# The mean of a SoLU layer taken from the activations on GpSimd instead of from the weights, with the transposes and loads around it moved

## The chip, the cores and the metric

One core of a Trainium2 chip. The metric is the device time of one execution in microseconds (us), lower is better. A time is the median of its runs, with the lowest and the highest behind it.

## The reference

All inputs have 8 batches, 8 heads, 576 rows, 64 columns per head; `w_in` is 512 x 1024, `w_out` 1024 x 512.

```python
scores = scale * q @ k.T                       # per batch and head, 576 x 576
thresh = max(scores) - tau                     # scores below it are dropped
attn   = softmax of what is left
x      = attn @ v                              # 4608 tokens x 512
h      = x @ w_in
u      = h * softmax(h)                        # "solu" in the original
mu, var = mean(u), mean((u - mu) ** 2)         # per token, over 1024
out    = ((u - mu) / sqrt(var + 1e-6) * g_ln) @ w_out
```

The point is `mu`. It can be taken from `u` (once per tile of 128 tokens), or from the weights: if each column of `g_ln * w_out` has its own mean taken off, a constant in `u` adds nothing to the product, and `mu` need not be subtracted at all.

## The kernel before

The kernel runs 144 **rounds**. Each does the scores of one block of 128 rows for two heads, and beside them one step of the rest. In the steady state four rounds make a cycle; I call them a, b, c and d:

- a: scores, x times `w_in` (first half), weights times v
- b: scores, x times `w_in` (second half), weights times v
- c and d: scores, u times `w_out` (two halves), transposes of the next batch's q and k

One cycle is one tile of 128 tokens, and there are 36. The last of them run after the last scores: the tail. These are the parts that the change touches (cuts marked by `...`):

```python
    def add_up(c): ...        # VectorE: total of w_out's chunks
    def mean(): ...           # TensorE: ones/1024 times total
    def center():
        for c in range(NC):
            nc.vector.tensor_tensor(out=w2[:, c], in0=w2[:, c], in1=totals[0], op=ALU.subtract)
    ...
    def scores(s, items):
        ps = [ps_mm.tile([P, 1024], F32, tag=f"s{h}", name="s_ps") for h in range(2)]
        ...
        for n, make, keep in items:     # transposes of q, k or u into the tiles' spare columns
            make(spare, x)
        for ks in (slice(SM, S), slice(0, SM)):
            ...                         # the scores themselves
    ...
    def ff_stats(t):
        ...
        for f in range(2):
            nc.vector.bn_stats(out=bs[:, f], in_=u[:, 512 * f : 512 * f + 512])
        nc.vector.bn_aggr(out=mv, in_=bs)
        # then six small GpSimd operations that make the row scale rs
    ...
    LAG_PV = 3      # weights times v is due three rounds after the scores
    ...
        # one round: scores(+transposes), maxes, ramp, exps | normalise, ff_stats |
        #            step with w_in or w_out | weights times v | block transposes to wT
```

`wT` holds the transposed softmax weights. VectorE turns 32 x 32 blocks, and eight DMA transfers put the blocks in place, so weights times v depends on a transfer. PSUM is full: two tiles for scores (their last 448 columns take transposes), and two tiles, here called the pair, for everything else.

Of the kernel before, what the change touches and what calls it, by code (L numbers as in the profile page):

```python
# [16 lines left out]
P = 128  # L17
# [3 lines left out]
def kernel(  # L21
# [225 lines left out]

    totals = []

    def add_up(c):  # L250
        if c == 1:
            totals.append(work.tile([P, DM], F32, tag="ob", name="total"))
        if c:
            total = totals[0]
            nc.vector.tensor_tensor(
                out=total, in0=total if c > 1 else w2[:, 0], in1=w2[:, c], op=ALU.add
            )

    def mean():
        total = totals[0]  # L260
        ones = work.tile([P, P], F32, tag="ob", name="ones")
        nc.gpsimd.memset(ones, 1.0 / DFF)
        tag, m = take("mean")
        nc.tensor.matmul(out=m[:, 0:DM], lhsT=ones, rhs=total, start=True, stop=True)
        nc.scalar.copy(out=total, in_=m[:, 0:DM])
        pairs_free.append(tag)

    def center():
        for c in range(NC):
            nc.vector.tensor_tensor(out=w2[:, c], in0=w2[:, c], in1=totals[0], op=ALU.subtract)  # L270



# [115 lines left out]
    def scores(s, items):  # L389
        b, kind, hp, r = slots[s]  # L390
        ps = [ps_mm.tile([P, 1024], F32, tag=f"s{h}", name="s_ps") for h in range(2)]

        spare = dict(enumerate(ps), base=S, eased=s <= NW)
        x = 0
        kept = []
        for n, make, keep in items:
            make(spare, x)
            kept.append((keep, x))
            x += n
        for ks in (slice(SM, S), slice(0, SM)):  # L400
            for h in range(2):
                for y in range(2):
                    if kind < 2:
                        d = pairs[b * NP + hp]
                        t = P * (2 * kind + r) + 64 * y
                        lhsT = d["qT"][ROWS[h], t : t + 64]
                    else:
                        d = pairs[b * NP + r + 2 * y]
                        lhsT = d["qe"][ROWS[h]]
                    nc.tensor.matmul(  # L410
                        out=ps[h][ROWS[y], ks], lhsT=lhsT, rhs=d["kT"][ROWS[h], ks],
                        start=True, stop=True,
                    )
        live[s] = dict(ps=ps, kept=kept, spare=spare)

# [73 lines left out]
    def attend(key):  # L489
# [3 lines left out]
        unit["y"] = take("pv")  # L493
        _, y = unit["y"]
        y = y.rearrange("p (u n) -> p u n", u=2)

        for e in range(2) if kind == 2 else [None]:
            for m in range(NK):
                for u in range(2):
                    d, h0 = source(b * NP + (hp if e is None else e + 2 * u))  # L500
                    for h in range(2):
                        if e is None:
                            to = y[ROWS[h], u, 0:P].rearrange("p (r g x) -> p g r x", r=2, g=2)
                            rhs = wT[ROWS[u], :, m, :, h]
                        else:
                            to = y[ROWS[h], u, 64 * e : 64 * e + 64].rearrange(
                                "p (g x) -> p g x", g=2
                            )
                            rhs = wT[ROWS[u], :, m, e, h]
                        nc.tensor.matmul(  # L510
                            out=to, lhsT=d["v"][ROWS[u], h0 + h, m], rhs=rhs,
                            start=m == 0, stop=m == NK - 1,
                        )

    def attended(key):
# [73 lines left out]

    def ff_stats(t):  # L590
        d = ffn[t]
# [4 lines left out]
        for f in range(2):  # L596
            nc.vector.bn_stats(out=bs[:, f], in_=u[:, 512 * f : 512 * f + 512])  # L597
        nc.vector.bn_aggr(out=mv, in_=bs)  # L598


# [11 lines left out]
    def u_item(t, f):  # L612
# [14 lines left out]

        return 4, make, keep


# [74 lines left out]
    for s, (b, kind, hp, r) in enumerate(slots):  # L705
        if r == 1:
            pv_due.append((s + LAG_PV, (b, kind, hp)))

# [5 lines left out]
    for i in range(NP, NPAIR):  # L714
        b, hp = divmod(i, NP)
        at = 8 + 2 * hp if i < 2 * NP - 1 else PER * (b - 1) + (6 + 3 * hp if hp < 3 else PER - 1)
        preps += [
# [7 lines left out]
    for b in range(1, B):  # L725
        r = PER * (b - 1)
        load_at.setdefault(r + 2, []).append(lambda b=b: load_qk(b, 0))
        load_at.setdefault(r + 8, []).append(lambda b=b: load_qk(b, 1))
        load_at.setdefault(r + 9, []).append(lambda b=b: load_v(b, 0))
        load_at.setdefault(r + PER + 6, []).append(lambda b=b: load_v(b, 1))  # L730

    with tc.manual_schedule():
# [6 lines left out]
        load_v(0, 0)  # L739
        load_v(0, 1)  # L740
        nc.sync.dma_start(out=g_rows, in_=g_ln.rearrange("(c p) -> c p", p=P))
# [4 lines left out]
        pieces = {r: x for x, r in enumerate(range(16))}  # L746
        whole = {0: 1, 1: 2, 3: 3}

# [8 lines left out]
        while True:  # L757
# [14 lines left out]
            busy = cur is not None or prev is not None  # L772
            items = []
            if more:
                room = SPARE
                if u_due and u_due[0][0] <= rnd:
                    _, t, f = u_due.pop(0)
                    items.append(u_item(t, f))
                    room -= 4
# [13 lines left out]
            elif u_due and u_due[0][0] <= rnd:  # L793
                for _, t, f in u_due:
                    ff_t(t, f)
                u_due = []
            if rnd in whole:
# [3 lines left out]
            if rnd - 1 in pieces:  # L801
                weight_c(pieces[rnd - 1])
            if pieces.get(rnd - 3) == 2 * NP + NC - 1:
                mean()
            for job in middle.pop(rnd, []):
# [12 lines left out]
            if due and (step is None or step[0] == "h") and len(pairs_free) > (step == ("h", 0)):  # L818
                attending = pv_due.pop(0)[1]
            if step == ("h", 0):  # L820
                ff_h(cur, 0, rnd + 1 < NS)
                quarter = 1
            elif step == ("h", 1):
# [3 lines left out]
                late.setdefault(rnd + 1, []).append(lambda t=cur: ff_mul(t))  # L827
                middle.setdefault(rnd + 3, []).append(lambda t=cur: ff_stats(t))
            elif step == ("o", 0):
# [3 lines left out]
            elif step == ("o", 1):  # L833
# [3 lines left out]
                if cur is not None:  # L837
                    u_due += [(rnd + 1, cur, 0), (rnd + 2, cur, 1)]
                prev, cur = cur, None
                quarter = 0  # L840
            if attending is not None:
                attend(attending)
                begin.setdefault(rnd + 1, []).append(lambda key=attending: attended(key))
                b, kind, hp = attending
# [10 lines left out]
            if rnd in pieces:  # L855
# [4 lines left out]
                if x + 1 < len(pieces):  # L860
                    weight_a(x + 1)
            x = pieces.get(rnd - 2, -1) - 2 * NP
            if x > 0:
                add_up(x)
            if pieces.get(rnd - 3) == 2 * NP + NC - 1:
                center()
                w2_done = True
            rnd += 1
# [33 lines left out]
```

## Time and profile before

| | before |
|---|---|
| time in the first measurement, us | 963.13 (962.52 to 965.56) |
| TensorE busy | 892.6 us, 93% of the span |
| VectorE, ScalarE, GpSimd busy | 72%, 61%, 49% |
| start of round 46 / rounds 46 to 142 / rest, us | 306.2 / 569.8 / 84.2 |
| mean length of a, b, c, d between rounds 46 and 141, us | 6.87, 6.88, 5.02, 4.98: cycle 23.75 |

The granted clock is the share of its full clock that TensorE's throttle let through. The waits of TensorE from 200 to 940 us complete what the prediction shows of the first 200. Columns: who waits (engine, tile, line), for whom, then us in total, number, longest; "issue" means that the profile names nobody. Tiles: `s_ps` holds scores, `h_ps` x times `w_in`, `pv` weights times v, `o_ps` u times `w_out`, `tp` and `tp_u` transposes, `uT` the turned u.

```profile
PE tp_u L638 <- ACT uT L641: 2.6, 3, 0.9
PE pv L510 <- issue: 1.5, 1, 1.5
PE s_ps L283 <- ACT w L439: 1.3, 2, 0.7
PE s_ps L410 <- issue: 0.5, 1, 0.5
PE s_ps L283 <- ACT uT L624: 0.3, 2, 0.2
```

### The profile page before, as it was taken

The numbers are of one execution on the slowest core, as the hardware profiler recorded it, in microseconds if no ns is written. First come the engines' busy times: TensorE is split into PE (matmuls) and PEld (weight loads), VectorE is DVE, ScalarE is ACT, GpSimd is POOL, SyncE is SP. The second block draws the span as 40 slices with busy tenths as digits, with TensorE's granted clock in tenths as the row PEclk, the third lists the DMA queues.
The fourth block names the chain that finished last, engine by engine and source line by source line (L and its number), as shares of the span: only waits on it lengthen the run. The fifth ranks groups of instructions, "written<-read, shape, count | busy, mean of one in ns | idle before, by whom it ended". The sixth has DMA issues, their size and how long they took to land. (4 is left out here: it accounts for less than half of the span.)

```text
span 964.4 us, 42893 instructions
## 1 busy us (share of the span) xinstructions
PE 892.6 (93%) x18583; PEld 647.8 (67%) x18583; DVE 692.1 (72%) x1298; ACT 593.0 (61%) x1291; POOL 473.2 (49%) x899
## 2 busy tenths in 40 slices
PE   4467678999999999999999999999999999999997
PEld 2334445678768777787777886778867887655543
DVE  4797976777767777777777777777777777777221
ACT  5676754677666666666666666666666666665111
POOL 2867665445544555445544454445544555554111
PEclk9587689999999999999999999999999999999999
DMA  9969625774678447874678546874668445744200
GB/s 238 255 192 196 159 68 150 172 190 116 150 176 201 115 114 175 202 165 117 160 176 191 121 119 164 202 163 115 170 154 206 110 118 131 163 112 111 61 22 22
DMA packets 87037, 143.31 MB, mean 149 GB/s; under 512 B 28985, under 2 KB 61761, under 8 KB 86849
## 3 DMA queue, kind: packets, MB, share of 16 engines
q1 hardware_dynamic: 85616, 138.60, 60.1%
q8 instruction: 147, 2.41, 1.1%
q10 hardware_dynamic: 1232, 1.97, 0.7%
q14 instruction: 42, 0.34, 0.1%
HBM read 46.14 MB, written 9.44 MB: 58 GB/s over the span
## 5 line engine op out<-in xcount | busy, mean ns | idle before, releaser
L439 ACT ACTIVATE w<-s_ps,nth 128x576 f32<-128x576 f32 x288 | 213.0, 741 | 238.6 <-DVE nth L430 202.5
L426 DVE TENSOR_REDUCE nm<-s_ps 128x1 f32<-128x576 f32 x288 | 216.4, 751 | 164.9 <-PE s_ps L410 164.1
L667 PE MATMUL o_ps<-w,uT 64*64 64x256 f32 x3968 | 232.2, 378 | 1.4 <-POOL mark L104 1.2
L667 PEld LDWEIGHTS o_ps<-w,uT 64*64 64x64 f32 x3968 | 195.0, 134 | 50.7 <-issue 15.7
L459 POOL TENSOR_SCALAR w<-w,sm 128x576 f32<-128x576 f32 x288 | 214.9, 758 | 14.4
L449 ACT ACTIVATE w<-w,ntau 128x576 f32<-128x576 f32 x288 | 219.4, 766 | 0.0
L562 PE MATMUL h_ps<-w,xh 64*64 64x512 f32 x1856 | 216.0, 592 | 0.0
L471 DVE STREAM_TRANSPOSE T<-w 128x576 f32<-128x576 f32 x288 | 206.5, 755 | 10.8 <-DMA wT<-T 8.4
L510 PEld LDWEIGHTS pv<-wT,v 64*64 64x64 f32 x5760 | 166.4, 137 | 49.9 <-issue 41.9
L510 PE MATMUL pv<-wT,v 64*64 64x128 f32 (+1 forms) x5760 | 169.4, 265 | 15.0 <-DMA wT<-T 13.5
L410 PE MATMUL s_ps<-kT,qT 64*64 64x64 f32 (+1 forms) x2048 | 170.4, 425 | 8.8 <-ACT w L439 7.2
L562 PEld LDWEIGHTS h_ps<-w,xh 64*64 64x64 f32 x1856 | 110.1, 134 | 91.1 <-issue 82.7
L456 POOL TENSOR_SCALAR sm<-sm 128x2 f32<-128x2 f32 x144 | 39.4, 274 | 264.1 <-ACT w L449 261.1
L457 POOL TENSOR_TENSOR sm<-sm,mone 128x2 f32<-128x2 f32 x144 | 103.4, 718 | 12.0
L430 DVE TENSOR_SCALAR nth<-nm,tau_t 128x1 f32<-128x1 f32 x288 | 61.7, 214 | 19.1
L410 PEld LDWEIGHTS s_ps<-kT,qT 64*64 64x64 f32 x2048 | 58.0, 141 | 12.6 <-ACT w L439 10.1
L581 ACT ACTIVATE u<-h_ps,hm 128x1024 f32<-128x1024 f32 x36 | 40.1, 1113 | 31.5 <-DVE hm L575 28.1
L575 DVE TENSOR_REDUCE hm<-h_ps 128x1 f32<-128x1024 f32 x36 | 43.0, 1193 | 17.6 <-PE h_ps L553 17.5
L449 ACT ACTIVATION_READ_ACCUMULATOR w<-w,ntau 128x1 f32 x288 | 55.2, 192 | 0.0
L104 POOL MEMSET mark<- 128x1 f32 x63 | 6.2, 98 | 97.7 <-PE o_ps L667 91.0
L283 PEld LDWEIGHTS s_ps<-ident,u 64*64 64x64 f32 x2016 | 46.8, 136 | 10.3 <-ACT qT L316 4.1
L283 PE MATMUL s_ps<-ident,u 64*64 64x64 f32 x2016 | 48.8, 221 | 4.8 <-ACT qT L316 2.4
(91 smaller groups left out, 775.8 us busy)
## 6 DMA issues: line engine op xcount, KB each, us to landing
wT<-T SPq DMA_DIRECT2D x576, 144.0 KB, 3.2
v<-in_v_dram SPq DMA_DIRECT2D x64, 256.0 KB, 5.6
out_dram<-ob SPq DMA_DIRECT2D x32, 256.0 KB, 3.7
q<-in_q_dram SPq DMA_DIRECT2D x15, 512.0 KB, 5.1
k<-in_k_dram SPq DMA_DIRECT2D x15, 512.0 KB, 6.8
raw<-in_moe_w_out_dram SPq DMA_DIRECT2D x8, 512.0 KB, 4.8
raw<-in_moe_w_in_dram SPq DMA_DIRECT2D x5, 512.0 KB, 6.4
v<-in_v_dram SPq DMA_DIRECT2D x32, 64.0 KB, 5.4
```

What stands on the lines that cost most here:

```text
L283: nc.tensor.matmul(out=spare[r][ROWS[y], to], lhsT=lhsT_of(r, y), rhs=ident[ROWS[r], ROWS[r]], start=True, stop=True,)
L410: nc.tensor.matmul(out=ps[h][ROWS[y], ks], lhsT=lhsT, rhs=d["kT"][ROWS[h], ks], start=True, stop=True,)
L426: nc.vector.tensor_reduce(out=nm, in_=ps[:, 0:S], axis=AX.X, op=ALU.max, negate=True)
L430: nc.vector.tensor_scalar(out=nth, in0=nm, scalar1=tau_t, scalar2=None, op0=ALU.add)
L439: nc.scalar.activation(out=w, in_=ps[:, 0:S], func=AF.Prelu, bias=d["nth"][x], scale=1.0, alpha=1.0e30,)
L449: nc.scalar.activation(out=w, in_=w, func=AF.Exp, bias=ntau, scale=1.0, accum_out=sm[:, x : x + 1])
L457: nc.gpsimd.tensor_tensor(out=sm, in0=sm, in1=mone, op=ALU.pow)
L459: nc.gpsimd.tensor_scalar(out=w, in0=w, scalar1=sm[:, x : x + 1], scalar2=1.0, op0=ALU.mult, op1=ALU.mult)
L471: nc.vector.transpose(out=T[:, :, r, h, :], in_=w)
L510: nc.tensor.matmul(out=to, lhsT=d["v"][ROWS[u], h0 + h, m], rhs=rhs, start=m == 0, stop=m == NK - 1,)
L562: mm = nc.tensor.matmul(out=h[ROWS[y], f], lhsT=x[ROWS[r], c, ROWS[y]], rhs=w1[ROWS[r], c, f], start=part == 0 and c == 0, stop=part == 1 ...
L667: mm = nc.tensor.matmul(out=o[ROWS[y], 512 * z : 512 * z + 256], lhsT=d["uT"][ROWS[r], c, ROWS[y]], rhs=w2[ROWS[r], c, 256 * z : 256 * z + ...
```

## The change

The intent: w_out needs no centring, so the first product with it can start earlier; GpSimd, which idles half the time, takes the mean from `u`; the scores come before the transposes, so that VectorE's maxima start earlier; half of the transposes of `u` share a PSUM tile with weights times v; early loads are spread. The diff, cut to its core:

```diff
-    def add_up(c): ...
-    def mean(): ...
-    def center(): ...
@@ def scores
-        (transposes of the items)
         for ks in (slice(SM, S), slice(0, SM)):
             ...
+        (transposes of the items)
@@ def ff_stats
         nc.vector.bn_aggr(out=mv, in_=bs)
+        (nc.gpsimd if beside else nc.vector).tensor_scalar(
+            out=u, in0=u, scalar1=mv[:, 0:1], scalar2=1.0, op0=ALU.subtract, op1=ALU.mult
+        )
@@ loads and first weights times v
-            pv_due.append((s + LAG_PV, (b, kind, hp)))
+            pv_due.append((s + LAG_PV + (s < 4), (b, kind, hp)))
-        (second batch's loads in rounds 2, 8, 9)
+        (second batch's loads in rounds 6, 10, 14; half of v in round 3, not at the start;
+         whole pairs prepared in rounds 0, 2, 4, not 0, 1, 3)
@@ the round
-                    u_due += [(rnd + 1, cur, 0), (rnd + 2, cur, 1)]
+                    u_due.append((rnd + 2, cur))
...
+            if attending is not None and step == ("h", 1) and more:
+                y = attend(attending)          # weights times v, now BEFORE the w_in half
+            elif turning is not None:
+                y = take("tp")
+            if y is not None:                  # second half of u into the same PSUM tile
+                turned = u_beside(turning, *y) if turning is not None else None
+                after()                        # ScalarE copies weights times v out
+                if turned:
+                    turned()                   # ScalarE and VectorE copy u out
             if step == ("h", 0): ...
```

Round b becomes: scores, first half of u, weights times v, second half of u, w_in. Before, one half of u stood ahead of the scores in round a and the other ahead of those in round b, and weights times v came last.

More of the change, by code (lines that the diff above doesn't have):

```diff
@@ L245, in weight_c @@
         nc.gpsimd.tensor_tensor(out=dst, in0=dst, in1=d["em"][0].bitcast(F32), op=ALU.mult)
-    totals = []
-    def add_up(c):
-        if c == 1:
-            totals.append(work.tile([P, DM], F32, tag="ob", name="total"))
-        if c:
-            total = totals[0]
-            nc.vector.tensor_tensor(
-                out=total, in0=total if c > 1 else w2[:, 0], in1=w2[:, c], op=ALU.add
-            )
-    def mean():
-        total = totals[0]
-        ones = work.tile([P, P], F32, tag="ob", name="ones")
-        nc.gpsimd.memset(ones, 1.0 / DFF)
-        tag, m = take("mean")
-        nc.tensor.matmul(out=m[:, 0:DM], lhsT=ones, rhs=total, start=True, stop=True)
-        nc.scalar.copy(out=total, in_=m[:, 0:DM])
-        pairs_free.append(tag)
-    def center():
-        for c in range(NC):
-            nc.vector.tensor_tensor(out=w2[:, c], in0=w2[:, c], in1=totals[0], op=ALU.subtract)
     SPARE = 7
@@ L393, in scores @@
         spare = dict(enumerate(ps), base=S, eased=s <= NW)
-        x = 0
-        kept = []
-        for n, make, keep in items:
-            make(spare, x)
-            kept.append((keep, x))
-            x += n
         for ks in (slice(SM, S), slice(0, SM)):
@@ L413, in scores @@
                     )
+        x = 0
+        kept = []
+        for n, make, keep in items:
+            make(spare, x)
+            kept.append((keep, x))
+            x += n
         live[s] = dict(ps=ps, kept=kept, spare=spare)
@@ L493, in attend @@
         unit["y"] = take("pv")
-        _, y = unit["y"]
+        y = unit["y"][1]
         y = y.rearrange("p (u n) -> p u n", u=2)
@@ L513, in attend @@
                         )
+        return unit["y"]
     def attended(key):
@@ L588, in ff_mul, with ff_stats @@
         pairs_free.append(d["tag"])
-    def ff_stats(t):
+    def ff_stats(t, beside):
         d = ffn[t]
@@ L628, in u_item, with u_beside, then @@
         return 4, make, keep
+    def u_beside(t, tag, y):
+        spare = {r: y[:, 512 * r : 512 * r + 512] for r in range(2)}
+        spare["base"] = P
+        _, make, keep = u_item(t, 1)
+        make(spare, 0)
+        def then():
+            for r in range(2):
+                keep(spare, 0, r)
+        return then
     def ff_t(t, f):
@@ L715 @@
         b, hp = divmod(i, NP)
-        at = 8 + 2 * hp if i < 2 * NP - 1 else PER * (b - 1) + (6 + 3 * hp if hp < 3 else PER - 1)
+        at = 9 + 2 * hp if i < 2 * NP - 1 else PER * (b - 1) + (6 + 3 * hp if hp < 3 else PER - 1)
         preps += [
@@ L726 @@
         r = PER * (b - 1)
-        load_at.setdefault(r + 2, []).append(lambda b=b: load_qk(b, 0))
-        load_at.setdefault(r + 8, []).append(lambda b=b: load_qk(b, 1))
-        load_at.setdefault(r + 9, []).append(lambda b=b: load_v(b, 0))
+        for at, job, hf in zip(
+            (2, 8, 9) if b > 1 else (6, 10, 14), (load_qk, load_qk, load_v), (0, 1, 0)
+        ):
+            load_at.setdefault(r + at, []).append(lambda b=b, job=job, hf=hf: job(b, hf))
         load_at.setdefault(r + PER + 6, []).append(lambda b=b: load_v(b, 1))
@@ L739 @@
         load_v(0, 0)
-        load_v(0, 1)
         nc.sync.dma_start(out=g_rows, in_=g_ln.rearrange("(c p) -> c p", p=P))
@@ L746 @@
         pieces = {r: x for x, r in enumerate(range(16))}
-        whole = {0: 1, 1: 2, 3: 3}
+        whole = {0: 1, 2: 2, 4: 3}
+        load_at[3] = [lambda: load_v(0, 1)]
         ready = []
@@ L773 @@
             items = []
+            turning = None
             if more:
@@ L776 @@
                 if u_due and u_due[0][0] <= rnd:
-                    _, t, f = u_due.pop(0)
-                    items.append(u_item(t, f))
+                    turning = u_due.pop(0)[1]
+                    items.append(u_item(turning, 0))
                     room -= 4
@@ L793 @@
             elif u_due and u_due[0][0] <= rnd:
-                for _, t, f in u_due:
+                t = u_due.pop(0)[1]
+                for f in range(2):
                     ff_t(t, f)
-                u_due = []
             if rnd in whole:
@@ L802 @@
                 weight_c(pieces[rnd - 1])
-            if pieces.get(rnd - 3) == 2 * NP + NC - 1:
-                mean()
+                w2_done = pieces[rnd - 1] == 2 * NP + NC - 1
             for job in middle.pop(rnd, []):
@@ L819 @@
                 attending = pv_due.pop(0)[1]
+            y = None
+            if attending is not None and step == ("h", 1) and more:
+                y = attend(attending)
+                after = lambda key=attending: attended(key)
+            elif turning is not None:
+                y = take("tp")
+                after = lambda tag=y[0]: pairs_free.append(tag)
+            if y is not None:
[3 more added lines that the diff above has]
+                    turned()
             if step == ("h", 0):
@@ L827 @@
                 late.setdefault(rnd + 1, []).append(lambda t=cur: ff_mul(t))
-                middle.setdefault(rnd + 3, []).append(lambda t=cur: ff_stats(t))
+                middle.setdefault(rnd + 3, []).append(
+                    lambda t=cur, beside=rnd + 3 < NS: ff_stats(t, beside)
+                )
             elif step == ("o", 0):
@@ L841 @@
             if attending is not None:
-                attend(attending)
-                begin.setdefault(rnd + 1, []).append(lambda key=attending: attended(key))
+                if y is None or turning is not None and step != ("h", 1):
+                    attend(attending)
+                    begin.setdefault(rnd + 1, []).append(lambda key=attending: attended(key))
                 b, kind, hp = attending
@@ L861 @@
                     weight_a(x + 1)
-            x = pieces.get(rnd - 2, -1) - 2 * NP
-            if x > 0:
-                add_up(x)
-            if pieces.get(rnd - 3) == 2 * NP + NC - 1:
-                center()
-                w2_done = True
             rnd += 1
```

## The prediction

> **What bounds the kernel now.** I read the page's slices first, then engine times in stretches of 20 us, then the waits of TensorE before and after 200 us, and last the order of instructions in a round. Columns below: stretch; busy us (count) of PE, PEld, DVE, ACT, POOL; granted clock; DMA share; GB/s.
>
> ```profile
> PE   4467678999999999999999999999999999999997
> PEclk9587689999999999999999999999999999999999
> DMA  9969625774678447874678546874668445744200
> ```
>
> ```profile
> 20.00:40.00 20.00, 9.35 (x169) 4.88 (x160) 17.39 (x33) 16.91 (x39) 15.94 (x20) 0.61 1.09 244
> ...
> 60.00:80.00 20.00, 10.75 (x234) 6.65 (x236) 19.21 (x36) 17.19 (x40) 16.64 (x22) 0.81 0.90 227
> ...
> 140.00:160.00 20.00, 16.38 (x272) 9.70 (x276) 15.36 (x26) 9.73 (x21) 11.22 (x20) 0.82 0.55 135
> ...
> 500.00:520.00 20.00, 19.93 (x460) 15.40 (x452) 14.24 (x28) 13.22 (x29) 9.40 (x20) 1.00 0.83 205
> ```
>
> There are two kernels in one. From 160 us on, TensorE is busy 20 of 20 us at clock 1.00, VectorE about 15, GpSimd about 10: TensorE alone sets the time. Before 160 us it is busy 101 of 160 us (sum of the eight stretches) at a clock of 0.6 to 0.9, VectorE reaches 19.2 of 20 us, and DMA is nearly full up to 100 us. The whole possible gain lies in these 160 us. Who TensorE waits for there (us, times, longest), from the waits up to 200 us:
>
> ```profile
> PE pv L510 <- DMA wT<-T: 13.5, 6, 4.9
> PE s_ps L283 <- ACT w L439: 7.6, 7, 3.9
> PE s_ps L410 <- ACT w L439: 7.2, 11, 1.7
> ...
> PE g_ps L176 <- DMA g_rows<-in_moe_g_ln_dram: 5.3, 1, 5.3
> ...
> PE mean L264 <- POOL ones L262: 2.7, 1, 2.7
> ```
>
> After 200 us the same view has 6.2 us in all, none of them on wT.
>
> **What the Trainium skill says.** "TensorE: Matmul & The Clock Gate", What's actually happening: after an idle window of about 3.4 us TensorE runs at half clock until it has been busy as long. The trace agrees in kind: clock 0.61 at 20 to 40 us, and one set of 72 weights-times-v matmuls takes some 3.9 us at 44 us against 2.23 us later. So a wait removed early pays a little twice. "Perfetto Trace Analysis", Optimization Strategy: with several regimes, look for the gaps inside the regime of interest; that is how I split this. "GPSIMD Engine Reference", Elementwise: about 1.03 cycles per element for simple bodies. This trace is slower: 758 ns for 576 elements, or 1.32 ns each, and I use that. "DMA: Bandwidth & Descriptors", Issuing engines are not separate DMA queues: all share 16 engines and interleave, so early loads delay the wT transfers; the 13.5 us above fit that.
>
> **The change, part by part.** Steady costs per piece, read from starts around 500 us: scores 0.97 us, half of u's transposes 0.47, half of x times w_in 3.43, weights times v 1.97, half of u times w_out 3.45. A cycle is four rounds: two with w_in and weights times v (6.84 us each), two with w_out (5.1 to 5.5).
>
> 1. Centring w_out goes. These are the groups:
>
> ```profile
> L270 DVE TENSOR_TENSOR w<-w,total 128x512 f32<-128x512 f32 x8 | 5.8, 799 | 1.8 <-ACT total L265 1.8
> L255 DVE TENSOR_TENSOR total<-total,w 128x512 f32<-128x512 f32 x6 | 4.1, 682 | 0.0
> L264 PE MATMUL mean<-total,ones 128*128 128x512 f32 x2 | 2.1, 1142 | 2.7 <-POOL ones L262 2.7
> ```
>
> VectorE loses 5.8 + 4.1 + 1.1 (first add) = 11.0 us, all before 150 us; TensorE loses 2.1 us and a 2.7 us wait. The first w_out product moves from round 19 to round 17 in the order of instructions.
>
> 2. Taking the mean from u is added 36 times: 32 on GpSimd, 4 on VectorE in the tail. One is 1024 x 1.32 ns = 1.35 us, together 43 us on an engine that is busy 49%. It is off the path if it ends before u is turned. In the round that starts at 500.66 us the statistics end at 506.1; 1.35 us more gives 507.5. The transposes now come after the next scores, near 508.3. It fits by about 0.8 us, more because scores (and so VectorE) start earlier.
>
> 3. Loads of the second batch go from rounds 2, 8, 9 to 6, 10, 14, half of v from the prologue to round 3, two whole-pair preparations one round later, the first products of weights and v a round later. This is aimed at the 13.5 and 5.3 us of DMA waits.
>
> 4. Transposes stand after the scores instead of before. TensorE's work is equal, but VectorE's maxima start 0.5 to 1 us earlier in rounds with transposes. Where the loop scores, maxima, ramp sets the early rounds (some seven), that is up to 1 us each.
>
> 5. Half of u's transposes goes beside weights times v, which now comes before w_in in that round. Same instructions, no TensorE time by itself.
>
> Sum for the start. Scores of round 0 start at 11.2 us, of round 16 at 124.2: 113 us. VectorE's floor is 2 x 0.751 + 2 x 0.214 + 2 x 0.755 + 0.903 + 0.814 + 0.494 + 0.483 = 6.1 us a round, 98 us for 16. Perfect overlap isn't to be had; I take 103, **-10 us**. Rounds 16 to 20 take 35.7 us now (124.2 to 159.9). In the new order they hold 5 scores, 4 halves of transposes, 3 weights times v, 2 halves with w_in, 2 with w_out and 1.3 us of other transposes: 27.7 us; with 3.3 us for waits and a clock below 1.00, 31. They also hold 5.5 us more work than before (one w_in half and one weights times v more). That is -4.7 and -5.5, **-10 us**. From round 45 on the four-round cycle has the same pieces in both kernels.
>
> Steady state: I take **+4 us** (see rivals). Tail: after the last scores TensorE runs the same 7 us products in both kernels; the subtraction on VectorE hides behind the 7 us product of the tile before (maximum to mul takes 3.7 us, statistics 1.5, subtraction about 1.1: 6.3), and a first whole turn of u costs an extra wait of 0.9: **+1 us**. Total -15: 963 - 15 = **948 us**.
>
> **The rivals.**
> A. *A new wait on wT in the steady state.* Weights times v in every fourth round is moved 3.43 + 0.47 = 3.9 us earlier against the transposes that feed it. The margin in the trace:
>
> ```profile
> 525.86 6.22 SPq L482 DMA_DIRECT2D wT<-T  x8
> ...
> 533.59 3.70 PE L562 MATMUL h_ps<-w,xe 64*64 64x512 f32 x32
> 537.02 2.23 PE L510 MATMUL pv<-wT,v 64*64 64x128 f32 x71
> ```
>
> The last of the eight issues starts at 531.5 and lands 3.4 us later, 534.9: 2.1 us of margin; a cycle later it is 3.5. Earlier scores give back 0.5 to 0.75. So 3.9 - 0.6 - (2.1 to 3.5) is 1.2 to -0.2 us per cycle, for 24 cycles -5 (none) to 29. I take a mean of 0.15 us, 4 us; at worst it eats the gain and leaves 965 to 970.
> B. *The start is bound by VectorE and ScalarE, and DMA waits hide behind them.* VectorE at 19.2 of 20 us speaks for it; its own waits (6.1 us on weights, 15.9 on scores up to 170 us) against. Then only -8, and 956.
> C. *GpSimd is late*, so transposes wait on the subtraction in every cycle: 0.5 us x 24 = 12 us. The 0.8 us margin speaks against.
> D. *Everything early falls away*, with a clock near 1.00 from 100 us: -27, 937.
>
> **Range and chances.** The start gives 8 to 27, steady state and tail take 0 to 13. 936 to 962. Faster by over 2% means below 943.9; that needs a start gain of 20 with no new wait: 0.30. Slower by 2% would need rival A at its worst: 0.03.
>
> **What would show it.** In the new profile: TensorE's waits on wT and g_rows before 200 us under 6 us (before 18.8); TensorE near 9 tenths from slice 6 instead of 7; round 21's scores at about 145 us; a group of 32 subtractions of some 1.35 us on GpSimd with no TensorE wait behind it; TensorE waits after 200 us at 5 to 10 us, on wT if anywhere. Waits of TensorE on wT over 15 us after 200 us would make me wrong to the slow side; a TensorE busy over 9 tenths by 100 us to the fast side.

## More of the kernel before

A round's start is the start of its first scores matmul in the trace, counted from the first instruction that does work, 0.24 us after the times in the views; "rest" in the tables by stretch ends with the last such instruction, 4.0 us before the execution ends. The profiled execution of the kernel before took 966.33 us, 3 us over its median, so a difference of a few us between profiled executions can be chance.

## The result, and the profile after

The changed kernel is correct and takes **1031.36 us** (1030.46 to 1033.65, 4 runs) against 962.83 (961.44 to 965.56, 4 runs) for the kernel before on the same chip. The ratio is 1.0712, 95% interval 1.0682 to 1.0742: slower by 7%.

The page of the changed kernel, busy tenths of TensorE and granted clock in 40 slices:

```profile
PE   4557789899899989999989999999999999898997
PEclk8678889999899999999999999999999999999999
```

There are now 8s of busy time and one 8 of the clock in the middle, where before stood 9s only. The groups of instructions, same page (busy us, mean ns; idle time of the engine before them):

```profile
L401 DVE TENSOR_REDUCE nm<-s_ps 128x1 f32<-128x576 f32 x288 | 216.1, 750 | 132.8 <-PE s_ps L258 102.1
...
L575 POOL TENSOR_SCALAR u<-u,mv 128x1024 f32<-128x1024 f32 x32 | 119.0, 3719 | 15.9 <-DVE mv L574 15.9
```

One subtraction on GpSimd takes **3.72 us**, where I had estimated 1.35. VectorE's maxima now wait for transposes (L258), which write the same PSUM tile; 79 of the 102.1 us fall in round b, where the transposes are those of u. TensorE's waits from 200 to 940 us, the five largest:

```profile
PE s_ps L258 <- POOL u L575: 26.7, 28, 3.2
PE s_ps L379 <- ACT w L414: 5.5, 14, 0.6
PE h_ps L538 <- issue: 4.4, 3, 3.0
PE pv L485 <- DMA wT<-T: 4.3, 6, 1.9
PE pv L258 <- issue: 4.1, 2, 3.7
```

The transposes of u wait for GpSimd in 28 rounds, 0.8 us in most of them. The longest of these waits costs more than itself, as the order of instructions around 262 us shows (start, length, engine, line):

```profile
262.46 3.72 POOL L575 TENSOR_SCALAR u<-u,mv 128x1024 f32<-128x1024 f32 x1 [0.46 <-DVE mv L574]
266.24 1.13 PE L258 MATMUL s_ps<-ident,u 64*64 64x64 f32 x32 [3.20 <-POOL u L575]
267.14 1.08 PE L258 MATMUL tp<-ident,u 64*64 64x64 f32 x32
268.00 5.36 PE L538 MATMUL h_ps<-w,xh 64*64 64x512 f32 x32
```

After an idle time of 3.20 us the same 32 matmuls with w_in take 5.36 us instead of the 3.70 that the prediction's lines show: the clock granted from 260 to 280 us was 0.83. Over 200 to 940 us, in stretches of 20 us, one minus the granted clock times 20 us sums to 13.8 us in the changed kernel, to 1.8 in the run with the addition below, and to 0 before. Of the 13.8 us, 6.8 come with the two waits for GpSimd of 3.2 us; 1.8 come with a wait on wT and 5.2 with two stops that have no named wait, of the kind explained further down.

Where the time came from, by stretch of the program (profiled executions, us):

| kernel | start of round 46 | rounds 46 to 142 | rest |
|---|---|---|---|
| before | 306.2 | 569.8 | 84.2 |
| changed | 312.3 | 628.2 | 87.2 |
| I had predicted (difference) | -20 | +4 | +1 |
| measured (difference) | +6.1 | +58.4 | +3.0 |

The steady loss lies in round b: means of a, b, c, d are 6.46, 9.51, 5.01, 5.21 us, the cycle 26.19 (before, between rounds 46 and 141: 6.87, 6.88, 5.02, 4.98, cycle 23.75; a has become shorter by 0.41 us, d longer by 0.23). The pieces of round b add up to 0.97 + 2 x 0.47 + 1.97 + 3.43 = 7.31 us.

### The profile page after: what moved, and what is told of

Its sections match the earlier page's. It is cut to its first block, busy times and chain, and to the rows that moved or that the text cites. A ratio compares the mean times of both kernels' runs of the same rounds, so it can differ in the third digit from the quotient of the medians.

```text
span 1031.9 us, 42774 instructions
## 1 busy us (share of the span) xinstructions
PE 918.9 (89%) x18553; PEld 686.4 (67%) x18553; DVE 687.7 (67%) x1289; ACT 590.5 (57%) x1287; POOL 590.3 (57%) x930
## 3 DMA queue, kind: packets, MB, share of 16 engines
q8 instruction: 146, 2.39, 1.0%
q10 hardware_dynamic: 1232, 1.97, 0.6%
## 5 line engine op out<-in xcount | busy, mean ns | idle before, releaser
L401 DVE TENSOR_REDUCE nm<-s_ps 128x1 f32<-128x576 f32 x288 | 216.1, 750 | 132.8 <-PE s_ps L258 102.1
L538 PE MATMUL h_ps<-w,xh 64*64 64x512 f32 x1856 | 227.5, 609 | 5.2 <-issue 4.4
L659 PEld LDWEIGHTS o_ps<-w,uT 64*64 64x64 f32 x3968 | 206.8, 133 | 11.3 <-issue 4.4
L379 PE MATMUL s_ps<-kT,qT 64*64 64x512 f32 (+1 forms) x2048 | 182.9, 426 | 32.7 <-ACT w L414 20.8
L485 PEld LDWEIGHTS pv<-wT,v 64*64 64x64 f32 x5760 | 170.0, 140 | 38.7 <-issue 23.2
L485 PE MATMUL pv<-wT,v 64*64 64x128 f32 (+1 forms) x5760 | 180.1, 270 | 16.3 <-DMA wT<-T 13.0
L538 PEld LDWEIGHTS h_ps<-w,xh 64*64 64x64 f32 x1856 | 114.3, 139 | 86.6 <-issue 68.2
L575 POOL TENSOR_SCALAR u<-u,mv 128x1024 f32<-128x1024 f32 x32 | 119.0, 3719 | 15.9 <-DVE mv L574 15.9
L379 PEld LDWEIGHTS s_ps<-kT,qT 64*64 64x64 f32 x2048 | 73.6, 138 | 58.6 <-ACT w L414 30.5
L603 DVE COPY uT<-pv 128x256 f32<-128x256 f32 x28 | 11.9, 425 | 86.5 <-ACT uT L603 86.5
L258 PEld LDWEIGHTS s_ps<-ident,u 64*64 64x64 f32 x992 | 18.6, 142 | 59.5 <-POOL u L575 59.0
```

What stands on the lines that cost most here:

```text
L379: nc.tensor.matmul(out=ps[h][ROWS[y], ks], lhsT=lhsT, rhs=d["kT"][ROWS[h], ks], start=True, stop=True,)
L401: nc.vector.tensor_reduce(out=nm, in_=ps[:, 0:S], axis=AX.X, op=ALU.max, negate=True)
L485: nc.tensor.matmul(out=to, lhsT=d["v"][ROWS[u], h0 + h, m], rhs=rhs, start=m == 0, stop=m == NK - 1,)
L538: mm = nc.tensor.matmul(out=h[ROWS[y], f], lhsT=x[ROWS[r], c, ROWS[y]], rhs=w1[ROWS[r], c, f], start=part == 0 and c == 0, stop=part == 1 ...
L575: (nc.gpsimd if beside else nc.vector).tensor_scalar(out=u, in0=u, scalar1=mv[:, 0:1], scalar2=1.0, op0=ALU.subtract, op1=ALU.mult)
L659: mm = nc.tensor.matmul(out=o[ROWS[y], 512 * z : 512 * z + 256], lhsT=d["uT"][ROWS[r], c, ROWS[y]], rhs=w2[ROWS[r], c, 256 * z : 256 * z + ...
```

## The experiments

Each is an edit of one of the two kernels or of an earlier experiment. The kernel before ran beside each group, with medians from 963.3 to 965.4 us. First theory: GpSimd's subtraction is the cause. Rival: the new order of round b is, because weights times v comes too early for its transfer. Both turned out to be true, and neither was enough.

### The subtraction by another engine, by another operation, or not at all

**On VectorE** (`e1_vector_sub`): `(nc.gpsimd if beside else nc.vector)` becomes `nc.vector`.

> The changed kernel, but the 32 subtractions go to VectorE (its four in the tail took 0.753 us each). Theory 1 (GpSimd's subtraction at 3.72 us makes u late, and everything lost follows from that): TensorE's waits on the subtraction vanish, clock back to 1.00 after 200 us, and the time falls to 940 to 955 us, as the prediction had it without the GpSimd term. Theory 2 (the new order itself loses: maxima that wait for u's transposes, weights times v that waits for wT): the time stays above 1000 us.

Measured: 1008.35 us (1004.46 to 1014.83), ratio 1.0449. From 200 to 940 us TensorE waits 0.2 us for the subtraction and 17.5 us on wT.

**Added, not subtracted** (`e2_gpsimd_add`): the mean is negated in place by a small VectorE operation.

```diff
+        if beside:
+            nc.vector.tensor_scalar(out=mv[:, 0:1], in0=mv[:, 0:1], scalar1=-1.0, scalar2=None, op0=ALU.mult)
-            out=u, in0=u, scalar1=mv[:, 0:1], scalar2=1.0, op0=ALU.subtract, op1=ALU.mult
+            out=u, in0=u, scalar1=mv[:, 0:1], scalar2=1.0, op0=ALU.add if beside else ALU.subtract, op1=ALU.mult
```

> The changed kernel, but GpSimd adds the negated mean (negated by one small VectorE operation) instead of subtracting the mean: same size, same tile, same place, same result. If the cost is the operation 'subtract', one takes about 1.35 us and the time is within 5 us of the run with VectorE. If it is the size of 1024, the place or the shared use of memory with VectorE, one still takes about 3.7 us and the time stays at 1031 us.

Measured: correct, 1001.33 us (998.54 to 1004.33), ratio 1.0370. The instructions on tile u (count, then shortest, median and longest in ns):

```profile
L579 POOL TENSOR_SCALAR u<-u,mv x32: 1117/1119/1127, 119.6 to 918.1; 128x1024 f32<-128x1024 f32 x32
```

**Multiplied** (`e3_gpsimd_mult`, wrong): `op0=ALU.mult`.

> Wrong result on purpose: GpSimd multiplies u by the mean and by 1.0, the pair of operations that its scaling of w uses, on 1024 columns. If duration follows the operation, one takes 1.35 us (1.32 ns a column, as for w) and the time is that of the runs with VectorE; if the size or the place is what costs, 3.7 us and 1031 us.

Measured: 999.00 us (997.42 to 1005.38), one operation 1.13 us.

**Subtraction without its second operation** (`e4_gpsimd_sub_alone`): `scalar2=None`, no `op1`.

> The changed kernel with the subtraction on GpSimd given without its second operation (times 1.0). Theory (subtract is the slow operation on GpSimd, 3.72 us against 1.12 us for add and multiply of the same size): one subtraction stays between 3 and 4 us and the total within 1% of the changed kernel, 1022 to 1040 us. Rival (it is the pair subtract-then-multiply that is slow): one takes 1.0 to 1.3 us, total about 1001 us.

Measured: correct, 1012.72 us (1006.10 to 1019.90), ratio 1.0518; in the view of tile u:

```profile
L575 POOL TENSOR_SCALAR u<-u,mv x32: 2854/2855/2857, 117.2 to 929.1; 128x1024 f32<-128x1024 f32 x32
```

The expectation was missed in its numbers on both sides: one takes 2.86 us, between the two theories' values. Both parts count. Subtract alone costs 2.86 us where add with a second multiply costs 1.12, and the second operation adds another 0.86 us to subtract.

**No mean at all** (`e5_no_mean`, wrong): the added lines of `ff_stats` are left out.

> Wrong result on purpose: the changed kernel with no subtraction of the mean anywhere. It shows what order, loads and the missing centring are worth with nothing added. Theory 1: 940 to 952 us, at most 5 us below the run with VectorE. Theory 2: above 1000 us.

Measured: 1005.86 us (1004.00 to 1011.53), ratio 1.0427.

What follows: replacing subtract by add gives back 30 of the 68.5 us, with all else equal but one small VectorE operation. With no operation on u at all the kernel is no faster than with the addition, so an addition of 1.12 us in this place costs nothing that shows. The other 38 us are left to the new order, since the moved loads alone (below) cost nothing. In the run with the addition, TensorE's largest wait from 200 to 940 us is

```profile
PE pv L485 <- DMA wT<-T: 15.6, 20, 1.4
```

and with no mean it is 18.8 us in 23 waits. That is my rival A. In the changed kernel itself it is only 4.3 us; the wait for GpSimd comes earlier in the round and hides it. With the addition the mean of round b falls from 9.51 only to 8.80 us.

### More time for wT

**Weights times v a round later** (`e8_add_pv_round_later`): the addition, and `LAG_PV = 4`.

> The mean is added negated on GpSimd, as in the run of that name (1001.3 us), and each weights-times-v is due one round later (lag 4 for 3), so the transfers into wT have a whole round more to land; the order inside a round is that of the changed kernel. Theory (the loss that stays when the subtraction is fast is TensorE waiting for wT in every fourth round, because weights times v now comes before x times w_in there): the TensorE waits on wT after 200 us fall from 15.6 us to under 2 us, the mean length of that fourth round falls from 8.80 us towards 7.3 us, about -1.3 us x 24 = -31 us, total 960 to 975 us. Rival (the order itself costs: transposes beside weights times v, bank changes, instruction fetch): the round stays at 8.3 us or more without any wait on wT, total 985 us or more. A second rival (wT has three buffers and a longer life makes the transfers wait for a buffer): wT issues start later and the waits only move.

Measured: correct, 981.62 us (977.65 to 983.42), ratio 1.0186. TensorE's waits from 200 to 940 us:

```profile
PE s_ps L379 <- ACT w L414: 8.2, 20, 0.6
PE pv L485 <- issue: 7.5, 5, 3.8
PE pv L258 <- issue: 2.6, 2, 2.4
```

No wait on wT is left, and 20 us are gone. The round that turns u has a median of 7.49 us, near its 7.31, but a mean of 8.13: a few rounds take 8 to 14 us. So the expectation (960 to 975) was missed, and what is left, beside 8.2 us of waiting for ScalarE, is waiting for nothing that the profile names ("issue"). One such place:

```profile
581.97 1.37 PE L485 MATMUL pv<-wT,v 64*64 64x64 f32 x67
...
587.15 2.29 PE L485 MATMUL pv<-wT,v 64*64 64x64 f32 x74 [3.81 <-issue]
```

TensorE stops in the middle of one group of matmuls for 3.8 us. The page lists a DMA queue for it:

```profile
q8 instruction: 146, 2.39, 1.0%
```

146 packets, 2.39 MB. The page counts 18,553 matmuls and as many weight loads of TensorE, so this is 64.4 bytes for each: q8 brings TensorE's own instructions, in packets of 16 KB, while the program runs. In this place the trace has no packet of q8 between 574.20 and 584.70 us; the next lands at 585.77, and TensorE goes on 1.4 us later. I looked for this signature in each trace from 200 to 930 us: at least 1.25 us from the start of one TensorE instruction to that of the next, with no wait named, that end 1.0 to 1.8 us after a packet of q8 landed.

```
kernel                              gaps   us in all   longest
before                                 1         1.7       1.7
changed                                5        12.0       3.9
addition                               6        11.6       3.7
addition, a round later                5        10.9       4.0
the last, whole transposes (below)     1         1.4       1.4
best version (below)                   1         1.7       1.7
```

Counting instructions tells what these gaps are. A packet of 16 KB holds 256 instructions of 64 bytes. In none of the 20 traces has TensorE at any moment started more than 449 instructions (every record of its own in the trace counts) plus 256 for each packet landed. At each gap of the table, but for two of the addition's six (3.0 us), it had started exactly 449 plus 256 for each packet before the one that let it go on: it had used up all that had been brought. Why those packets came late the traces don't say.

The new order puts 32 + 72 + 32 small matmuls of u and v behind the 16 of the scores: with weight loads 304 instructions, or 19.5 KB at 64 bytes, before the first slow matmul with w_in. Before, w_in stood between them.

**Fewer instructions** (`e17_e8_whole_transposes`): half of u turned by four transposes of 128 x 128 instead of 32 matmuls of 64 x 64.

```diff
-                turn(spare, x + c, lambda r, y: d["u"][ROWS[r], o + 64 * y : o + 64 * y + 64])
+                nc.tensor.transpose(out=at(spare, c), in_=d["u"][:, o : o + P], identity=ident)
```

> The run with a round of lag in the order of the changed kernel (981.6 us), with each half of u turned by four transposes of 128 x 128 instead of sixteen times two of 64 x 64: 8 instructions (weight loads counted) for 64, each half 0.1 us longer. Theory (TensorE runs out of instructions in the dense stretch): stalls over 1.3 us that end 1.0 to 1.7 us after an instruction packet landed fall from four (9.3 us in all after 200 us, the longest 4.0) to one or two under 2 us; total 968 to 977 us. Rival (they are waits for data that the profile does not name): stalls as before, total 981 to 988 us.

Measured: correct, 973.89 us (972.21 to 974.33), ratio 1.0110. The gaps fall from five to one, with 133 packets of q8 for 146: this again speaks for the supply of instructions against a wait for data. But the 7.7 us are not these gaps. The round that turns u keeps its mean of 8.1 us, because its median grew from 7.49 to 7.96: each half takes 0.1 us more, as expected (0.59 us against 0.46 and 0.50), and the pieces around them take longer too. The gain lies mainly in round d, 5.32 to 5.07 us, where TensorE's wait for ScalarE (8.2 us in the view above) is now

```profile
PE s_ps L379 <- ACT w L414: 1.7, 4, 0.6
```

The edit also changes which engine copies which chunk, so it is not a test of one thing alone, and what shortened this wait is not shown.

### Undoing the order, and what came instead

**Weights times v after w_in again** (`e9_add_pv_after_w_in`), with the second half of u in a PSUM tile of the pair. The main line of the edit (the condition at the round's end goes with it):

```diff
-            if attending is not None and step == ("h", 1) and more:
+            if False:
```

> The mean is added negated on GpSimd (1001.3 us with the order of the changed kernel); the one part of the new order undone is that weights times v stands after x times w_in again, the second half of u's transposes going to a PSUM tile of its own. Theory (wait on wT): the same as a round of lag, waits on wT after 200 us under 2 us, fourth round 7.0 to 7.5 us instead of 8.80, total 955 to 970 us. Rival (transposes after the scores cost VectorE's maxima and so the scores of the next round): the round stays over 8 us, total over 985 us.

Measured: correct, **1022.99 us** (1020.38 to 1025.05), far from the 955 to 970 expected. No wait on wT is left; in its place, from 200 to 940 us:

```profile
PE pv L485 <- DVE uT L608: 33.5, 27, 1.7
```

Weights times v now takes the PSUM tile that held u, and VectorE's copy out of it stands late in VectorE's queue.

**w_in between** (`e11_add_w_in_between`): scores, half of u, w_in, weights times v, other half of u beside them.

> GpSimd adds the negated mean (1001.3 us in the order of the changed kernel). The fourth round is now scores, half of u, x times w_in, weights times v, other half of u beside them: w_in stands between the groups of small matmuls, wT gets 3.4 us more, and weights times v wait for no PSUM tile that VectorE still reads (the wait of 33.5 us that spoilt the run with weights times v after w_in). Theory (the loss of the order is waiting for wT, plus TensorE running out of instructions in the dense stretch of small matmuls): waits on wT and on uT after 200 us under 3 us, stalls without a named releaser over 1.3 us at most two, fourth round 7.3 to 7.6 us, cycle 23.7 to 24.2, total 958 to 972 us. Rival (turning u after the scores, with VectorE's maxima waiting for it, costs by itself): cycle stays above 24.8 us, total above 980 us.

Measured: correct, 1009.76 us (1008.46 to 1013.41), again a miss. The same view:

```profile
PE o_ps L664 <- DVE uT L608: 21.7, 23, 1.4
PE h_ps L538 <- POOL mark L104: 16.3, 25, 0.7
```

Now u times w_out takes that tile too early, and w_in waits for a fence (`mark`, a one-column write by GpSimd that keeps matmuls in order) that stands in GpSimd's queue behind the addition. With a round of lag more (`e12_e11_lag4`, `LAG_PV = 4`):

> The run before with weights times v due one round later. Theory: the early rounds wait no longer on wT (8 to 10 us before 200 us fall under 3), the steady cycle is that of the run before (23.7 to 24.2), the tail 3 to 5 us longer; total 948 to 962 us, perhaps faster than the kernel before. Rival: the round of lag gives nothing at the start because VectorE sets it; total equals that of the run before plus 4 us.

Measured: 1006.83 us (1004.49 to 1009.70). The same two waits, 24.4 and 16.5 us.

**The order of before, and the mean from u** (`e13_before_mean_from_u`): no centring, `ff_stats` a round earlier, the addition on GpSimd, nothing else.

> The kernel before with the mean taken from u alone: no centring of w_out, statistics of u one round earlier (so that they come before the first half's transposes), GpSimd adds the negated mean; order, loads and lag are those of before. Theory (moving the mean is itself cheap and the loss came from the operation chosen and from the order): steady cycle 23.7 to 24.0 us, start of round 46 at 300 to 306 us, total 952 to 964 us. Rival (36 more passes over u cost a per cent or more wherever they stand): total 970 us or more.

Measured: correct, 1020.13 us (1018.21 to 1022.72), another miss:

```profile
PE s_ps L256 <- POOL u L575: 48.7, 28, 2.0
```

The statistics are last in VectorE's queue in round d, GpSimd adds after them, and the transposes at the head of round a want u 1.7 us before that is done. With a round of lag (`e14_e13_lag4`):

> The run before with weights times v due one round later. Theory (wT waits at the start are worth their 13 us): TensorE waits on wT before 200 us under 3 us, start of round 46 by 8 to 15 us earlier than before, tail 3 to 5 us longer, total 942 to 956 us. Rival (VectorE sets the start): total within 4 us of the run before.

Measured: 1010.53 us (1008.02 to 1014.84); the same wait, 45.1 us.

So each of four placements had waits of 16 to 49 us: on a transfer, on VectorE, on VectorE and GpSimd, on GpSimd. The open question was whether one is always there.

### All the named waits removed

**u in the scores' tiles** (`e15_u_in_scores_tile`): from the run with the addition. Seven of the eight chunks of u are turned after the scores of round b into the scores' tiles (7 x 64 columns, all that is spare), the eighth in round c. Weights times v is last again and shares no tile with u. The small operations for the row scale move a round later, so that only the addition is ahead of the fence.

```diff
+    U_PARTS = (range(0, 7), range(7, NC))
-                    u_due.append((rnd + 2, cur))
+                    u_due += [(rnd + 2, cur, 0), (rnd + 3, cur, 1)]
+                middle.setdefault(rnd + 4, []).append(lambda t=cur: ff_rs(t))
```

> GpSimd adds the negated mean; seven chunks of u are turned after the scores in the scores' PSUM tile, the eighth a round later; weights times v after x times w_in, as before; the chain of small GpSimd operations on the row scale moves a round later. Theory (each loss so far was one named wait, not the mean itself): TensorE waits after 200 us under 12 us in all, cycle 23.6 to 24.2 us, start as in the other runs without centring (round 46 at 298 to 304 us), total 950 to 964 us. Rival (a wait is always there): cycle over 24.6, total over 975 us.

Measured: correct, 994.18 us (988.89 to 996.46). Yet another wait:

```profile
PE o_ps L666 <- ACT xh L507: 27.5, 23, 1.7
```

With a round of lag (`e16_e15_lag4`):

> The run before with weights times v due a round later. Theory (early waits on wT go, tail 3 to 5 us longer): round 46 at 292 to 297 us, total 945 to 958 us, faster than the kernel before by 0.5 to 2%. Rival: no gain from the lag, total as the run before.

Measured: 985.77 us (981.64 to 987.26); the wait is 25.9 us. The order of instructions shows why: ScalarE's copy of weights times v (xh) is queued behind its exponential of the next u, and that waits for the last chunk of the old u, which has one buffer.

**The copy first** (`e18_e15_exp_after_copy`, and with the lag `e19_e16_exp_after_copy`):

```diff
-                late.setdefault(rnd, []).append(lambda t=cur: (ff_max(t), ff_exp(t)))
+                late.setdefault(rnd, []).append(lambda t=cur, r=rnd + 1: (
+                    ff_max(t), begin.setdefault(r, []).append(lambda: ff_exp(t))
+                ))
```

> The run with u turned in the scores' tile (994.2 us), with ScalarE's exponential of u issued after the copy of weights times v instead of before it. Theory (one named wait at a time): the TensorE wait for ScalarE's copy (29.8 us after 200 us) falls under 4 us, cycle from 25.24 to 23.7 to 24.1 us, total 960 to 970 us. Rival (another wait takes its place): cycle stays over 24.6 us, total over 980 us.

> The same with weights times v due a round later (985.8 us). Theory: cycle from 25.01 to 23.6 to 24.0 us, start of round 46 at 290 to 294 us, total 948 to 960 us, faster than the kernel before by up to 1.5%. Rival: total over 975 us.

Measured: 965.75 us (964.69 to 966.60), ratio 1.0004, and **953.62 us** (952.11 to 955.25), ratio 0.9879 with interval 0.9844 to 0.9913; both correct. TensorE's waits of the second, 200 to 940 us:

```profile
PE tp_u L637 <- ACT uT L640: 3.7, 5, 0.9
PE s_ps L379 <- ACT w L414: 1.6, 4, 0.6
PE pv L485 <- issue: 1.4, 1, 1.4
```

It has 7.9 us of waiting in all, against 6.2 in the kernel before, with the mean taken on GpSimd and no centring. The gain of 1.2% is clear of noise. The run without the lag has a cycle of 24.19 us and four gaps by the signature above (8.4 us in all); with it 23.87 and one. Why a round of lag lessens them I did not find out.

### The loads and the lag by themselves

**Before, with the change's moves of loads only** (`e10_before_loads`):

> The kernel before with only the change's moves of loads: second batch's loads in rounds 6, 10, 14, half of v in round 3, two whole-pair preparations a round later, the first two weights-times-v a round later. Theory (these loads are hidden behind VectorE and ScalarE, as the small gain of 2 to 6 us by round 16 in all runs so far says): start of round 16 moves by 0 to -4 us, total 958 to 964 us, same. Rival (my prediction: transfers are what the start waits for): round 16 moves by -8 us or more, total 950 to 955 us.

Measured: 961.58 us (960.03 to 964.51), ratio 0.9989, interval 0.9954 to 1.0023. That cannot be told from zero. In the profiled executions round 16 starts at 116.3 instead of 124.2 us, more than I expected of it, and the end comes 4.7 us earlier; the medians keep 1.7 us of that, since the profiled execution of the kernel before was a slow one.

**Before, with the lag only** (`e20_before_lag4`, `LAG_PV = 4`):

> The kernel before with weights times v due one round later and nothing else changed. If the lag alone makes the gain of the best version (953.6 us), this takes 950 to 956 us. If the early product with w_out, which the missing centring allows, is needed as well, the lag alone gives 0 to 5 us: 958 to 966 us, with round 46 starting after 298 us (286.2 in the best version, 306.2 before).

Measured: 958.71 us (955.12 to 963.86), ratio 0.9955, interval 0.9920 to 0.9991. By stretches, with the others (us):

| kernel | start of round 46 | rounds 46 to 142 | rest |
|---|---|---|---|
| before | 306.2 | 569.8 | 84.2 |
| addition (e2) | 303.1 | 605.3 | 84.8 |
| addition, lag (e8) | 292.1 | 594.6 | 88.9 |
| best without lag (e18) | 294.2 | 579.8 | 84.7 |
| best (e19) | 286.2 | 572.8 | 88.2 |
| before, lag only (e20) | 295.2 | 568.3 | 89.5 |

The lag gives 11 us by round 46 and takes 5 back in the tail, because work is only put off. The rest of the best version's gain, 9 us by round 46 (295.2 less 286.2), comes with the mean from u, the order that goes with it and the moved loads; the loads alone bring round 46 forward by 5.5 us in their profiled execution, so how it divides is not shown. The last two kernels' medians are only 0.5% apart (958.71 and 953.62, on different chips). The intervals of their ratios to the kernel before, up to 0.9913 and from 0.9920, just do not overlap.

## Why the prediction was wrong

The direction was wrong: 948 us predicted, with a range to 962, and 1031 measured. By its own steps:

1. **Bound and reading.** Right: TensorE alone sets the steady state. What I didn't draw from it is that with 6.2 us of waits in 740 us every new delay beyond a margin adds to the time. I looked for gain in the first 160 us and sized the risk in the other 800 with one margin for each engine. Three slips: the clock was 1.00 in the first 20 us, and 0.59 to 0.93 from there to 160 us; rounds c and d last 5.02 and 4.98 us in the mean, not 5.1 to 5.5 (no sum rests on it); and the range's upper end, 962, is narrower than its own terms, since 963 - 8 + 13 is 968.
2. **Subtraction of 1.35 us (step 2 of the sum, and rival C).** This failed most. I scaled the duration from a multiplication of 576 elements and treated subtraction as the same. Measured: 3.72 us; add and multiply take 1.12 and 1.13, even below the estimate. The 0.8 us of margin became a lack of 1.6 us by the same working (0.8 + 1.35 - 3.72), and rival C, put at 12 us and set aside, became 26.7 us of waits and at least 6.8 us of lost clock. Swapping the operation alone gave 30 us back.
3. **Rival A, wT.** The mechanism was right and the size was not. The working gave 1.2 to -0.2 us per cycle; I then took 0.15, below the middle of my own interval, 0.5. In the run with the addition the named waits of rounds 46 to 142 are 15.0 us, 0.6 for each of 24 cycles, and the median of round b falls by 1.0 us when the lag takes them away (8.46 to 7.49). The 4 us should have been 15 to 24. My worst case with it, 965 to 970 us, was still too low, since it had no place for steps 2 and 4.
4. **"Same instructions, no TensorE time by itself" (step 5).** This failed in a way I had no term for. With small matmuls next to each other TensorE stops until a late packet of its instructions has landed: 12.0 us in five gaps, against 1.7 us in one before. The count of instructions shows that it had none left in each of them, and fewer instructions removed four of five. That the packing of small matmuls is what makes the packets late fits all this; no run tests it alone.
5. **Start, -20.** The changed kernel reached round 46 later by 6.1 us, with the addition earlier by 3.1: GpSimd's delay and the wT waits act there as well. The best version arrives 20 us earlier, but that agreement is luck: it takes a lag, which I hadn't counted on, for 11 of them, and 4 come back in the tail.
6. **Loads (step 3).** I expected TensorE's waits on wT and on g_rows before 200 us to fall from 18.8 under 6 us. They are 8.7 us on wT, and g_rows' 5.3 became 3.9 on ScalarE. The loads alone bring the waits on wT to 7.1 us, and give 1.7 us of the median, within the noise: closer to rival B than to the sum.
7. **Scores before transposes (step 4).** The maxima did not start earlier. From round 46 on they start 1.2 to 1.3 us after the round's first scores matmul in all four rounds of the kernel before; in the changed kernel 1.3 us in round a, but 2.8, 2.2 and 2.1 in b, c and d, the rounds with transposes: more than the 0.5 us by which the scores now come sooner. The profile names the transposes in the same PSUM tile as what they wait for (102.1 us).
8. **Tail, +1.** It is +3.0 us. Not looked into.

The signs that I gave to tell by: round 21 at 145 us (156.3 measured), subtractions of 1.35 us with no TensorE wait behind them (3.72 and 26.7 us), waits after 200 us of 5 to 10 us on wT if anywhere. All three failed at the first look. (TensorE's 9 tenths did come one slice earlier, as I had said.) The sign for the slow side, over 15 us on wT, was hidden behind GpSimd and came out once GpSimd was fast.

The sum of the 68.5 us, as the runs took it back, in this order: 30.0 with add for subtract; 19.7 with a round for wT (some 5 of which the lag alone gives); 7.7 with whole transposes. Another order would split them otherwise. The best version goes another way from the addition on, and comes 11 us under the kernel before once its named waits are placed; 5 of these the lag alone gives.

## What to carry to other kernels

Take the duration of a new operation from the same operation in a trace, not from a neighbour with the same shape; if there is none, measure it alone first, since here one word (add for subtract) was worth 3%. In a kernel where the bounding engine waits 1% of its time, a move needs its whole round laid out: the transfer that feeds it, the PSUM tile it takes, and the place in the queue of each engine that frees that tile; four placements that I thought safe cost 16 to 49 us of waiting by one of these. And spread groups of small matmuls between long ones, because back to back they came with the gaps in the supply of instructions here.

## What the Trainium skill lacked or had wrong

- "GPSIMD Engine Reference", 3.1 Elementwise, gives about 1.03 cycles per element for simple bodies and names no arithmetic operation on one input that differs. For add and multiply the runs agree in kind: 0.81 ns per element, from 1119 ns for 1024 and 758 ns for 576. Subtract of 1024 elements by a per-row value takes 2855 ns, and 3719 ns with a second operation, on the same engine and in the same place. On VectorE the subtraction takes 753 ns with the second operation and 752 without.
- "Trainium Architecture — The Big Picture", The software stack, says that instructions have 64 bytes (the trace agrees: 2.39 MB for 37,106 TensorE instructions) and that their streams are brought by DMA at load time. The trace has 146 packets of 16 KB on an instruction queue throughout the run, and TensorE stops of up to 4.0 us that end 1.0 to 1.8 us after one landed. "Runtime: NRT & Kernel Launch", Instruction fetch mechanics, does describe blocks of 16 KB that are brought while the program runs, but takes this to be hidden; in the changed kernel five such gaps add up to 12.0 us. No page says that a dense stretch of small matmuls can run dry.
